# Attention in blocks that may span two units: the value bank and the spare bank change roles from unit to unit

## The chip, the cores and the metric

One Trainium2 chip, one of its cores. The metric is the device time of one execution in microseconds (us); the lower the better. A core has a matrix engine (TensorE, PE in the profile; its weight loads are listed apart as PEld), a vector engine (VectorE, DVE), an activation engine (ScalarE, ACT), GpSimd (POOL) and the engine that issues most transfers (SyncE, SP). Each runs its own instructions in their order; they meet at semaphores. Matmuls write to PSUM, which has 8 banks of 128 partitions x 512 floats.

## The reference

The program normalises 2048 rows of 512 numbers, runs full attention with 32 heads of 16 dimensions over them, runs a SwiGLU feed-forward network over the same normalised rows, and uses the network's output as a gate on the attention's.

```python
xn = layernorm(x)                                   # 2048 x 512
q, k, v = split(xn @ wqkv)                          # 32 heads of 16
p = softmax(q @ k.T * 16 ** -0.5)                   # 2048 x 2048 for each head
s = (p @ v) @ wo
g = silu((silu(xn @ w_gate) * (xn @ w_up)) @ w_down)   # inner width 1792
return x + s * g
```

## The kernel before

All of it is one function, `tile_block`, whose instructions are issued in a hand-written order. A first stage (some 163 us) normalises the rows, makes queries, keys and values and stores them in DRAM, in two parts each, a rounded value and the rest, so that single-pass float32r matmuls keep float32 accuracy. Then come the 32 **units** of attention. A unit is one group of four heads (of 8) and one block of 512 queries (of 4); `u = 4 * group + block`. It runs over 16 key tiles (`kt`) of 128 keys. For each key tile there are two **pairs** of heads. A pair's scores are two matmuls of 50 rows, one on the upper and one on the lower half of the array, which run side by side.

- A **direct** pair writes both halves to one of two score tiles in PSUM (`scored`); ScalarE takes the exponential from there (line 966). Two score tiles mean that the third pair waits until the first's exponential is done.
- A **copied** pair writes one half at a time to a single spare PSUM bank (`spare_bank`, which is `acc[1]`); VectorE copies each half to SBUF (lines 1022 and 1028) and ScalarE takes the exponential there, at the end (line 1036). Its two halves are the events A and B of the block's order.

Between the scores the matrix engine does **fills**: `fill(1)` takes the next step of the feed-forward network (later of the output projection) from a queue, two matmuls of 64 rows side by side into the banks `bankx` and `banky` (line 188, later 381). The exponentials of a pair take longer than its scores, and the fills use that time.

The order is cut in **blocks**. A block has so many key tiles, so many fills and, behind them, one section of `values` (line 410): the products of the block's exponentials with the values, four heads side by side in the array's four column groups, added up over the unit in the PSUM bank `acc[0]`. The blocks' fills (`sizes`) are 24 or 21, as the network's chains of 3 x 8, 3 x 7 come, so that a chain ends with its block; 88 of the entries belong to the network, the last 8 to the output projection. Before the change a block belongs to one unit. There are three blocks for each unit, 96 in all, with 5, 6 and 5 key tiles as a rule (the six where the fills are many). To make it come out even, two of the 24-step chains are parted into two blocks of 12 fills and 4 tiles, one at units 22/23 and one at units 30/31. Their first two pairs are issued ahead (`begin`), inside the previous block's values, so that the values come in two pieces there: 100 sections of values for 96 blocks.

`events(n, f, ...)` writes down a block's order of fills (F), direct pairs (D) and copied halves (A, B), for instance `DDFAFFFFDFFBDFFFDFFAFDFFFDFBFDFFFDFFFD` for 6 tiles and 24 fills: 10 direct and 2 copied pairs. There are four common forms, named here by fills/direct/copied: 24/10/2 (6 tiles), 24/9/1 (5 tiles), 21/8/2 (5 tiles), 21/9/3 (6 tiles). `run` issues the block. Small VectorE work (rounding of weights and the like) waits in the list `chores` and is issued between the copies where there is room.

When a unit's last values are done, `finish` has VectorE transpose `acc[0]` to SBUF (`turn`, line 421), invert the sums (line 426) and scale (line 430). It is queued after the second pair of the next block. Nothing but the next unit's own values, a whole block later, needs the bank that the transpose reads. SP loads the queries of unit u+1 when unit u begins (`load_q`, `load_shift`), and the next group's keys and values in a ring of five buffers as its chunks come free.

After the last block the projection of the last queries ends the kernel.

Of the kernel before, what the change touches and what calls it, by code (L numbers as in the profile page):

```python
# [9 lines left out]
F32 = mybir.dt.float32  # L10
# [36 lines left out]
PARTED = (22, 23)  # L47
# [5 lines left out]
def tile_block(ctx: ExitStack, tc: tile.TileContext, x, wqkv, wo, w_gate, w_up, w_down, out):  # L53
# [301 lines left out]
    def out_splits():  # L355
        for b, c in {early: ((0, 0), (0, 1), (0, 2)), early + 2: ((1, 0), (1, 1)), early + 3: ((1, 2), (2, 0)),
                     early + 4: ((2, 1),), early + 5: ((2, 2),)}.get(now, ()):
# [48 lines left out]
    def values(u, kts, probs):  # L406
        for kt in kts:
            v = vst[(u // NB * NB + kt // CT) % RING]
            for h in range(4):
                mm(acc[0][h * 32:h * 32 + DH + 1], v[:, kt % CT, h * (DH + 1):(h + 1) * (DH + 1)],  # L410
                   probs[kt, h // 2][:, h % 2], start=kt == 0, stop=kt == KT - 1, skip_group_check=True)

    def normalise(u, first, last, between=None):
        g, b = divmod(u, NB)
        n = last - first
        turned = {}
        dst = on[b][:, first:last].rearrange("p (c s d) -> p c s d", s=2, d=DH)[:, :, g % 2]

        def turn():
            turned[0] = late.tile([P, TB], F32, tag="o", name="o")[:, :n]  # L420
            dve.transpose(turned[0], acc[0][:, first:last])
# [74 lines left out]
    blocks, opened = [], []  # L496
    for u in range(units):
        opened.append(len(blocks))
        if u == 0:
            ns = [4, 6, 6]  # L500
        elif u in PARTED or u >= units - 2:
            ns = ([4, 6, 6] if u % 2 else [6, 6, 4])
        else:
            ns = [5] * 3
            far = sizes[len(blocks):len(blocks) + 3]
            ns[far.index(max(far)) if far[1] < max(far) else 1] = 6
        kt = 0
        for n in ns:
            blocks.append((u, kt, n))
            kt += n  # L510

    def events(n, f, ahead):
        length = 2 * n - ahead + f
        need = 2 * n - max(2, (10 * length + 46) // 40)
        fit = (10 * length + 55) // 112
        copied = n - 3 if ahead else max(0, min(need, fit)) if now else 0
# [3 lines left out]
        ds = [] if ahead else [0, 1]  # L520
        ds += [(0.5 if ahead else 7) + gap * i for i in range(direct - 2)]
        cs = [((0.3 if ahead else 2.2) + far * i, "AB"[i % 2]) for i in range(2 * copied)]
# [421 lines left out]
    spare_bank = acc[1]  # L944
# [24 lines left out]
    begun = {}  # L969

    def begin(u, first, n):
        for j in range(2):
            begun[first, j] = scored(u, j, first, j)

    def run(u, first, n):
        nonlocal lower
        f = sizes.pop(0) if sizes else 0
        direct, todo = events(n, f, len(begun))
# [3 lines left out]
        if now >= early and f != pair // 2:  # L982
# [3 lines left out]
        pairs = [(kt, j) for kt in range(first, first + n) for j in range(2)]  # L986
        straight, copies = pairs[:direct], pairs[direct:]
        probs, waiting, turned_in = {}, [], []

# [5 lines left out]
        done = len(begun)  # L995
        if done:
            probs.update(begun)
            begun.clear()
            unit_end()
        copying = [t + 1.5 for t, e in todo if e in "AB"]  # L1000
        final = max(at for at, (_, e) in enumerate(todo) if e == "F")
        free = 0
        for at, (t, e) in enumerate(todo):
# [4 lines left out]
            elif e == "D":  # L1008
                probs[straight[done]] = scored(u, done % 2, *straight[done])
# [3 lines left out]
            elif e == "A":  # L1013
# [3 lines left out]
                kt, j = copies.pop(0)  # L1017
                waiting.append((kt, j))
                scores(u, spare_bank, kt, j, 0)
                lower = True  # L1020
                probs[kt, j] = ppool.tile([P, 2, TB], F32, tag="pr", name="pr")
                dve.tensor_copy(probs[kt, j][:, 0], spare_bank)  # L1022
                free = copying.pop(0) + 3
            else:
                kt, j = waiting[-1]
                scores(u, spare_bank, kt, j, 1)
                lower = False
                dve.tensor_copy(probs[kt, j][:, 1], spare_bank)  # L1028
# [6 lines left out]
        for kt, j in waiting:  # L1035
            act(probs[kt, j], probs[kt, j], AF.Exp, scale=0.25)  # L1036
# [5 lines left out]
        kts = range(first, first + n)  # L1042
        if now + 1 in begins:
            values(u, kts[:-1], probs)
            begin(*blocks[now + 1])
            values(u, kts[-1:], probs)
        else:
            values(u, kts, probs)

    for now, (u, first, n) in enumerate(blocks):  # L1050
        g, b = divmod(u, NB)
        if first == 0 and 0 < u < units - 1:
            load_q(u + 1)
            load_shift(u + 1)
        if now == 3 or first == 0 and 0 < g < NG - 1 and b == 0:
            load_k(g + 1, 0)
            load_v(g + 1, 0)
        run(u, first, n)
# [6 lines left out]
        if b == NB - 1 and g + 1 < NG:  # L1065
            for c in range(NB - 1):
                if first < (c + 1) * CT <= first + n:
                    load_k(g + 1, c + 1)
                    load_v(g + 1, c + 1)
        if first + n == KT and u + 1 < units:  # L1070
            ends.append(partial(finish, u))
# [7 lines left out]
    outs = (score[0][:, 0], score[1][:, 0], spare_bank, bankx)  # L1079
# [73 lines left out]
```

## Time and profile before

| | |
|---|---|
| median of 3 runs | 1393.43 us (1393.23 to 1393.66) |
| the profiled execution's own time | 1393.85 us |
| its span, first to last instruction | 1392.1 us |
| TensorE busy | 1386.0 us (100%) |
| ScalarE busy | 1087.5 us (78%) |
| VectorE busy | 757.7 us (54%) |
| granted TensorE clock | 0.999 |

The profiled execution is 0.42 us above the median of the runs, and its span is 1.75 us shorter than its own time. The page gives busy time for each engine, the chain of work that ended last, and the costliest groups of instructions. Since matmuls are pipelined and two or four of them run side by side, a TensorE that is busy all the time can still lose time between its instructions; what counts is when each section of the order starts. The chain of waits, in order of time, lists each section of values as one piece with its start, so that the distance from one section to the next is the length of a block.

### The profile page before, as it was taken

Reading aid. Unit: us, or ns where it says so; the run is one execution under the profiler, and the core shown is the slowest. Engines: PE = TensorE matmul, PEld = TensorE weight load, DVE = VectorE, ACT = ScalarE, POOL = GpSimd, SP = SyncE. Lnnn points to the kernel's source line nnn. Section 1 sums busy time; section 2 is a strip of 40 time slices with the busy share of each in tenths; the row PEclk is TensorE's granted clock in tenths of the full one; section 3 lists DMA queues with packets and bytes.
Section 4 is the critical chain, followed back from the end, with each engine's and each line's share of the span. In section 5 each row is a group of like instructions: output and inputs, shape, how many; then the busy total and the mean of one; then the engine's idle time right before and its main releaser. Section 6 shows DMA issues by size and latency. Waiting matters only on the chain.

```text
span 1392.1 us, 27644 instructions
## 1 busy us (share of the span) xinstructions
PE 1386.0 (100%) x11193; PEld 850.6 (61%) x11193; DVE 757.7 (54%) x1295; ACT 1087.5 (78%) x1245; POOL 74.4 (5%) x92
## 2 busy tenths in 40 slices
PE   9999999999999999999999999999999999999998
PEld 7777756655655655565556566555655565565665
DVE  6675555355545653555456544564555446556544
ACT  6753678778888877887887787788888887788785
POOL 4200200000000000000000000000000000000222
PEclk9999999999999999999999999999999999999999
DMA  7778641043534511144524402347124212224323
GB/s 228 269 247 267 175 109 43 13 113 88 127 91 115 122 44 36 47 127 98 131 62 108 104 13 63 84 128 163 50 66 116 54 27 70 82 81 151 125 82 138
DMA packets 126954, 148.15 MB, mean 106 GB/s; under 512 B 12524, under 2 KB 79340, under 8 KB 126052
## 3 DMA queue, kind: packets, MB, share of 16 engines
q1 hardware_dynamic: 121620, 125.79, 33.9%
q0 software_dynamic: 4912, 20.12, 3.9%
q8 instruction: 90, 1.47, 0.4%
q14 instruction: 44, 0.36, 0.1%
q10 hardware_dynamic: 288, 0.39, 0.1%
HBM read 106.68 MB, written 39.58 MB: 105 GB/s over the span
## 4 chain that ended last, share of the span: by engine, by line
PE 88%; ACT 0%; DVE 0%; issue 0%; DVEq 0%
PE acc L410 32%; PE bankx L188 23%; PE score L960 17%; PE banky L188 10%; PE acc L960 3%; PE bankx L381 2%; PE banky L381 1%; ACT pr L966 0%; PE acc L1090 0%; PE bankx L1090 0%; PE score L1090 0%; DVE y L1097 0%; DVE y L1103 0%; DVEq L1149 0%
## 5 line engine op out<-in xcount | busy, mean ns | idle before, releaser
L966 ACT ACTIVATE pr<-score 128x1024 f32<-128x1024 f32 x859 | 812.5, 1031 | 222.6 <-PE score L960 221.3
L410 PE MATMUL acc<-pr,vst 128*17 128x512 f32 x4096 | 459.0, 593 | 0.0
L960 PE MATMUL score<-qst,kst 50*128 50x512 f32 x1718 | 394.4, 413 | 0.1
L188 PE MATMUL bankx<-fx,guh 64*128 64x512 f32 x896 | 332.0, 393 | 0.1
L188 PE MATMUL banky<-fx,guh 64*128 64x512 f32 x896 | 323.3, 393 | 0.0
L410 PEld LDWEIGHTS acc<-pr,vst 128*17 128x17 f32 x4096 | 110.1, 97 | 290.8 <-issue 269.2
L960 PEld LDWEIGHTS score<-qst,kst 50*128 50x128 f32 x1718 | 175.1, 184 | 143.8 <-issue 70.6
L1022 DVE COPY pr<-acc 128x512 f32<-128x512 f32 x165 | 114.1, 692 | 186.8 <-PE acc L960 183.8
L188 PE MATMUL bankx<-wd,hh 64*128 64x512 f32 x672 | 199.5, 392 | 0.0
L188 PE MATMUL banky<-wd,hh 64*128 64x512 f32 x672 | 197.0, 391 | 0.0
L188 PEld LDWEIGHTS bankx<-fx,guh 64*128 64x128 f32 x896 | 166.5, 186 | 21.1 <-issue 2.6
L188 PE MATMUL banky<-fx,gul 64*128 64x512 f32 x448 | 175.5, 392 | 0.0
L188 PE MATMUL bankx<-fx,gul 64*128 64x512 f32 x448 | 175.2, 391 | 0.0
L188 PEld LDWEIGHTS banky<-fx,guh 64*128 64x128 f32 x896 | 166.4, 186 | 5.2
L1036 ACT ACTIVATE pr<-pr 128x1024 f32<-128x1024 f32 x165 | 168.8, 1077 | 0.0
L1028 DVE COPY pr<-acc 128x512 f32<-128x512 f32 x165 | 114.0, 691 | 75.1 <-PE acc L960 61.8
L188 PEld LDWEIGHTS bankx<-wd,hh 64*128 64x128 f32 x672 | 125.0, 186 | 12.1
L241 DVE SCALAR_TENSOR_TENSOR ga<-th,bankx 128x512 f32<-128x512 f32 x56 | 38.5, 688 | 171.5 <-ACT th L240 171.4
L960 PE MATMUL acc<-qst,kst 50*128 50x512 f32 x330 | 130.8, 396 | 0.0
L188 PEld LDWEIGHTS banky<-wd,hh 64*128 64x128 f32 x672 | 124.9, 186 | 3.8
L188 PEld LDWEIGHTS bankx<-fx,gul 64*128 64x128 f32 x448 | 83.6, 187 | 10.9
L188 PEld LDWEIGHTS banky<-fx,gul 64*128 64x128 f32 x448 | 83.5, 186 | 2.7
(186 smaller groups left out, 1297.9 us busy)
## 6 DMA issues: line engine op xcount, KB each, us to landing
gur<-in_B_w_gate_dram SPq DMA_DIRECT2D x56, 256.0 KB
gur<-in_B_w_up_dram SPq DMA_DIRECT2D x56, 256.0 KB
wdr<-in_B_w_down_dram SPq DMA_DIRECT2D x56, 256.0 KB
kst<-k_d SPq DMA_DIRECT2D x192, 64.0 KB
qst<-q_d SPq DMA_DIRECT2D x192, 64.0 KB
fx<-xt_d SPq DMA_DIRECT2D x24, 512.0 KB
q_d<-parts SPq DMA_DIRECT2D x16, 512.0 KB
k_d<-parts SPq DMA_DIRECT2D x16, 512.0 KB
```

What stands on the lines that cost most here:

```text
L188: mm(banks[i], lhs[halves[i]], rhs[halves[i]], start=start, stop=stop)
L241: dve.scalar_tensor_tensor(ga, th, 1.0, bankx, op0=ALU.add, op1=ALU.mult)
L381: mm(banks[k], lhs[b, c][a][halves[h], (j + k) * P:(j + k + 1) * P], fx[halves[h], w, c], start=swap == i == 0, stop=i == 3 * n - 1, skip_ ...
L410: mm(acc[0][h * 32:h * 32 + DH + 1], v[:, kt % CT, h * (DH + 1):(h + 1) * (DH + 1)], probs[kt, h // 2][:, h % 2], start=kt == 0, stop=kt = ...
L960: mm(bank, k[r, j, kc * P:(kc + 1) * P], qst[u % 2][r, j], start=True, stop=True)
L966: act(pr, score[slot], AF.Exp, scale=0.25)
L1022: dve.tensor_copy(probs[kt, j][:, 0], spare_bank)
L1028: dve.tensor_copy(probs[kt, j][:, 1], spare_bank)
L1036: act(probs[kt, j], probs[kt, j], AF.Exp, scale=0.25)
```

## The change

- **Blocks** are made from the list of fills alone: 6 tiles where there are 24 fills, otherwise 5, with some of the sixes turned to fives so that the sum is 512 tiles; the first three and the last three have 4, 6 and 6. A block takes its tiles from wherever the previous one stopped, so that it may hold the last tiles of one unit and the first of the next: `blocks` is now a list of lists of parts `(u, first, n)`. Neither chain is parted any more: 94 blocks, 25 of which span two units. `begin` and `PARTED` are gone.
- **Banks**: unit u adds up its values in `acc[u % 2]`, and the spare bank for copied pairs is the other one, chosen by the unit with which the block begins. So the bank that held a finished unit's values is the spare bank of the next blocks.
- **finish** issues the transpose at once instead of putting it in the list of chores, since the first copied half of that block writes over the bank.
- **events**: in the block behind a unit's end (`late`) the first copied half stands 5 steps in instead of 2.2: `DDFFFAFF...` instead of `DDFAFFFF...`. The special case for parted blocks is gone.
- The loads of a unit's successor's queries and of the next group's first keys go out behind the block in which the unit begins, where that block spans two units. The splits of two output operands come in one block instead of two.

```diff
-PARTED = (22, 23)
...
-                mm(acc[0][h * 32:h * 32 + DH + 1], v[:, kt % CT, h * (DH + 1):(h + 1) * (DH + 1)],
-                   probs[kt, h // 2][:, h % 2], start=kt == 0, stop=kt == KT - 1, skip_group_check=True)
+                mm(acc[u % 2][h * 32:h * 32 + DH + 1], v[:, kt % CT, h * (DH + 1):(h + 1) * (DH + 1)],
+                   probs[u, kt, h // 2][:, h % 2], start=kt == 0, stop=kt == KT - 1, skip_group_check=True)
...
-            dve.transpose(turned[0], acc[0][:, first:last])
+            dve.transpose(turned[0], acc[u % 2][:, first:last])
...
-        chores.extend(normalise(u, 0, TB))
+        (_, turn), *rest = normalise(u, 0, TB)
+        turn()
+        chores.extend(rest)
...
-    sizes[3 * PARTED[0] + 2:3 * PARTED[1]] = [3 * DC // 2] * 2
...
-    sizes += [6 * (DT - 1), pair, pair, pair, pair // 2, pair // 2, pair, pair]
-    begins = tuple(3 * u + i for a in (PARTED[0], units - 2) for u, i in ((a, 2), (a + 1, 0)))
...
+    sizes += [6 * (DT - 1)] + [pair] * (2 * (NB - 1))
+
+    ns = [6 if f == max(sizes) else 5 for f in sizes]
+    ns[:3] = ns[-3:] = [4, 6, 6]
+    long = [i for i, n in enumerate(ns) if n == 6 and 3 <= i < early]
+    over = sum(ns) - units * KT
+    for i in range(over):
+        ns[long[(2 * i + 1) * len(long) // (2 * over)]] = 5
+
+    blocks, opened = [], {}
+    u = kt = 0
+    for n in ns:
+        parts = []
+        while n:
+            some = min(n, KT - kt)
+            if not kt:
+                opened[u] = len(blocks)
+            parts.append((u, kt, some))
+            n -= some
+            kt += some
+            if kt == KT:
+                u, kt = u + 1, 0
+        blocks.append(parts)
...
-        cs = [((0.3 if ahead else 2.2) + far * i, "AB"[i % 2]) for i in range(2 * copied)]
+        ds = [0, 1] + [7 + gap * i for i in range(direct - 2)]
+        cs = [((5 if late else 2.2) + far * i, "AB"[i % 2]) for i in range(2 * copied)]
...
-        direct, todo = events(n, f, len(begun))
+        n = sum(some for _, _, some in parts)
+        direct, todo = events(n, f, bool(ends))
...
+        spare_bank = acc[(parts[0][0] + 1) % 2]
...
-        if now + 1 in begins:
-            values(u, kts[:-1], probs)
-            begin(*blocks[now + 1])
-            values(u, kts[-1:], probs)
-        else:
-            values(u, kts, probs)
...
+        for u, first, some in parts:
+            values(u, range(first, first + some), probs)
...
+        if len(parts) > 1:
+            queries_ahead(parts[1][0])
```

How the instructions move is seen at three places. The first is TensorE's order at unit 22's parted block; `score` are the two score tiles, `acc_80` and `acc_81` the banks `acc[0]` and `acc[1]`, `pr` the exponentials, `vst` the values, `kst` and `qst` keys and queries. Before:

```order
L960 MATMUL score_8971<-qst_557,kst_8975 128x512 x2
L410 MATMUL acc_80<-pr,vst_554 17x512 x8
L410 MATMUL acc_80<-pr,vst_8976 17x512 x12
L960 MATMUL score_8970<-qst_557,kst_8979 128x512 x2
L960 MATMUL score_8971<-qst_557,kst_8979 128x512 x2
L410 MATMUL acc_80<-pr,vst_8976 17x512 x4
L188 MATMUL bankx<-fx,guh 128x512
```

Two pairs of the next block stand between the values of the fifth tile and those of the sixth. With the change, at the end of unit 22 (block 67):

```order
L963 MATMUL score_8971<-qst_8987,kst_549 128x512 x2
L409 MATMUL acc_80<-pr,vst_8980 17x512 x16
L409 MATMUL acc_81<-pr,vst_550 17x512 x8
L963 MATMUL score_8970<-qst_8987,kst_549 128x512 x2
L963 MATMUL score_8971<-qst_8987,kst_549 128x512 x2
L187 MATMUL bankx<-fx,guh 128x512
```

The section of values is in one piece again, and in that one piece unit 22's last four tiles go to `acc_80` and unit 23's first two to `acc_81`.

The second place is TensorE's order behind the end of unit 1, from the end of the values on. Before, with the values in `acc_80` and the spare bank `acc_81`:

```order
L410 MATMUL acc_80<-pr,vst_554 17x512 x4
L960 MATMUL score_8970<-qst_557,kst_553 128x512 x2
L960 MATMUL score_8971<-qst_557,kst_553 128x512 x2
L188 MATMUL bankx<-wd,hh 128x512
L188 MATMUL banky<-wd,hh 128x512
L960 MATMUL acc_81<-qst_557,kst_8975 128x512
```

That is a block inside a unit; before the change the block behind a unit's end has the same order. With the change, behind unit 1's end (unit 1 in `acc_81`, the first tile of unit 2 in `acc_80`):

```order
L409 MATMUL acc_80<-pr,vst_550 17x512 x4
L963 MATMUL score_8970<-qst_557,kst_549 128x512 x2
L963 MATMUL score_8971<-qst_557,kst_549 128x512 x2
L187 MATMUL bankx<-wd,hh 128x512
L187 MATMUL banky<-wd,hh 128x512
L187 MATMUL bankx<-wd,hh 128x512
L187 MATMUL banky<-wd,hh 128x512
L187 MATMUL bankx<-wd,hh 128x512
L187 MATMUL banky<-wd,hh 128x512
L963 MATMUL acc_81<-qst_557,kst_553 128x512
```

The first copied half has moved behind three fills, and it writes the bank that VectorE has to read first.

The third place is VectorE's order at the same sort of block, behind unit 2's end. Before:

```order
L421 STREAM_TRANSPOSE o<-acc_80 128x512
L426 RECIPROCAL rl<-o 128x16
L1022 COPY pr<-acc_81 128x512
L430 TENSOR_TENSOR on_8997<-o,rl 128x16x16
```

With the change:

```order
L420 STREAM_TRANSPOSE o<-acc_80 128x512
L425 RECIPROCAL rl<-o 128x16
L1018 COPY pr<-acc_80 128x512
L429 TENSOR_TENSOR on_8997<-o,rl 128x16x16
```

VectorE's own order is the same; only the bank of the copy is now the one that the transpose has read.

More of the change, by code (lines that the diff above doesn't have):

```diff
@@ L489, in tile_block, with events @@
     sizes = sizes[1:]
-    sizes[3 * PARTED[0] + 2:3 * PARTED[1]] = [3 * DC // 2] * 2
     early = len(sizes)
     pair = 6 * DT
-    sizes += [6 * (DT - 1), pair, pair, pair, pair // 2, pair // 2, pair, pair]
-    begins = tuple(3 * u + i for a in (PARTED[0], units - 2) for u, i in ((a, 2), (a + 1, 0)))
[L496 to L502, printed above, removed]
-        else:
[L504 to L513, printed above, removed]
+    sizes += [6 * (DT - 1)] + [pair] * (2 * (NB - 1))
[19 more added lines that the diff above has]
+        blocks.append(parts)
+    def events(n, f, late):
+        length = 2 * n + f
         need = 2 * n - max(2, (10 * length + 46) // 40)
         fit = (10 * length + 55) // 112
-        copied = n - 3 if ahead else max(0, min(need, fit)) if now else 0
+        copied = max(0, min(need, fit)) if now else 0
         direct = 2 * n - copied
@@ L967, in scored, with run @@
         return pr
[L969 to L975, printed above, removed]
+    def run(parts):
         nonlocal lower
-        f = sizes.pop(0) if sizes else 0
-        direct, todo = events(n, f, len(begun))
+        f = sizes.pop(0)
+        n = sum(some for _, _, some in parts)
+        direct, todo = events(n, f, bool(ends))
         if now == 0:
@@ L981, in run @@
                 todo.insert(0, todo.pop(max(i for i, (_, e) in enumerate(todo) if e == "F")))
-        if now >= early and f != pair // 2:
+        if now >= early:
             behind = [i for i, (_, e) in enumerate(todo) if e == "F"][f // 2]
@@ L1064, in tile_block @@
             load_shift(1)
[L1065 to L1071, printed above, removed]
+        for u, first, some in parts:
+            g, b = divmod(u, NB)
+            if b == NB - 1 and g + 1 < NG:
+                for c in range(NB - 1):
+                    if first < (c + 1) * CT <= first + some:
+                        load_k(g + 1, c + 1)
+                        load_v(g + 1, c + 1)
+            if first + some == KT and u + 1 < units:
+                ends.append(partial(finish, u))
+        if len(parts) > 1:
+            queries_ahead(parts[1][0])
     fill(total)
@@ L1078, in tile_block @@
     lo = one.tile([P, D], F32R, tag="th", name="rl")
-    outs = (score[0][:, 0], score[1][:, 0], spare_bank, bankx)
+    outs = (score[0][:, 0], score[1][:, 0], acc[units % 2], bankx)
     half = TB // 2
```

52 lines of the change are left out of this document (25 added, 27 removed).

## The prediction

> **What bounds the kernel now.** I read the page first, for the engine that is never idle and for the chain, then the chain of waits in order of time, for the length of each block.
>
> ```profile
> span 1392.1 us, 27644 instructions
> ...
> PE 1386.0 (100%) x11193; PEld 850.6 (61%) x11193; DVE 757.7 (54%) x1295; ACT 1087.5 (78%) x1245; POOL 74.4 (5%) x92
> ...
> PEclk9999999999999999999999999999999999999999
> ...
> PE 88%; ACT 0%; DVE 0%; issue 0%; DVEq 0%
> ...
> L966 ACT ACTIVATE pr<-score 128x1024 f32<-128x1024 f32 x859 | 812.5, 1031 | 222.6 <-PE score L960 221.3
> ```
>
> TensorE is busy throughout, at the full clock, and nearly the whole chain is its own. ScalarE waits 221 us for scores, VectorE is idle for 46%. Since matmuls overlap, "busy" hides lost time; I look for it in when things start. First the pace of the order inside a block, from TensorE's timeline:
>
> ```profile
> 353.49 0.39 PE L960 MATMUL score<-qst,kst 50*128 50x512 f32 x2
> ...
> 356.28 0.40 PE L960 MATMUL score<-qst,kst 50*128 50x512 f32 x2
> ```
>
> Between these two pairs lie three rounds of three fills and a pair, 12 steps in 2.79 us: **0.2325 us for a step** (a fill or a pair; a copied half counts a half). Then the values and the blocks, from the chain of waits (start, length, what; x8 is one key tile, x40 five, x48 six):
>
> ```profile
> 241.35 4.42 PE acc L410 x40
> 254.00 5.27 PE acc L410 x48
> ...
> 536.58 4.42 PE acc L410 x40
> 548.54 4.42 PE acc L410 x40
> ...
> 665.03 4.42 PE acc L410 x40
> 677.60 5.27 PE acc L410 x48
> ...
> 729.14 4.42 PE acc L410 x40
> 741.80 4.42 PE acc L410 x40
> ...
> 997.42 5.27 PE acc L410 x48
> 1011.39 5.27 PE acc L410 x48
> 1057.19 5.27 PE acc L410 x48
> 1071.15 5.27 PE acc L410 x48
> ...
> 1300.02 5.27 PE acc L410 x48
> 1314.25 5.28 PE acc L410 x48
> ...
> 1360.50 5.28 PE acc L410 x48
> ```
>
> and, for the parted chain, the same view from 1025 us on:
>
> ```profile
> 1025.36 4.42 PE acc L410 x40
> 1029.78 0.66 PE score L960 x3
> 1030.44 0.98 PE acc L410 x8
> 1031.42 0.43 PE bankx L188
> ...
> 1035.95 2.70 PE acc L410 x24
> ```
>
> One tile of values takes 0.98, six take 5.27: 0.86 each and 0.12 for the section. From the start of one section to the next runs a section of values and the steps of the next block; what is left when 0.86 a tile and 0.2325 a step are taken off is the block's **fixed part**:
>
> - 24/10/2: 1011.39 - 997.42 = 13.97, less 5.16 and 36 steps (8.37): 0.44. With a six before and behind it (1057.19 to 1071.15) it is 13.96, so sixes in a row cost nothing more.
> - 24/9/1: 12.66 - 4.30 - 34 steps (7.91) = 0.45. 21/8/2: 11.96 - 4.30 - 31 steps (7.21) = 0.45.
> - 21/9/3: 12.65 and 12.57, less 4.30 and 33 steps (7.67): 0.68 and 0.60, mean 0.64.
> - 24/10/2 in the output projection: 14.23 - 5.16 - 8.37 = 0.70.
> - The parted chain at units 22/23: 1025.36 to 1057.19 is 31.83 us and holds 14 tiles (12.04) and 20 + 20 + 36 steps (17.67). That leaves 2.12, of which one whole block has 0.44: 1.68 for the two small ones.
> - The parted one at units 30/31: 1314.25 to 1360.50 is 46.25, with 20 tiles (17.20) and 36 + 20 + 20 + 36 steps (26.04): 3.01, less two whole blocks at 0.70: 1.61.
>
> So the kernel is TensorE's work plus some 0.45 us a block.
>
> **The change, part by part.** The work itself stays: 512 tiles, 1024 pairs, the same fills; only their order changes. By the planner's own lists there are now 94 blocks with 94 sections of values, none parted, none 21/9/3; behind block 2 the network's part has 39 of 24/10/2, 32 of 21/8/2 and 15 of 24/9/1.
>
> - Two parted chains become whole blocks: 1.68 - 0.44 = 1.24 and 1.61 - 0.70 = 0.91, saved. One of the last stage's blocks now has no copied pair, which the trace shows only ahead of the first values; its fixed part lies between 0.31 (two bare pairs, 0.66 less two steps, and a section's 0.12) and 0.70. I take 0.70, that of its neighbours, whose banks turn over in the same way.
> - Five blocks of 21/9/3 become 21/8/2: 5 x (0.64 - 0.45) = 0.95, saved.
> - The rest of the blocks swap forms with the same 0.44 to 0.45: nothing.
> - 859 direct pairs become 855 and 165 copied ones 169. TensorE's steps are the same. VectorE gets 8 copies of 0.69 more, 5.5 us over the span in 46% idle time; without that cover they would cost those 5.5.
> - Transpose and spare bank: the first copied half behind a unit's end now waits for the transpose. What stands there before:
>
> ```profile
> 348.32 0.61 PE L410 MATMUL acc<-pr,vst 128*17 128x512 f32 x4
> 348.87 0.73 PE L960 MATMUL score<-qst,kst 50*128 50x512 f32 x4
> 349.43 0.40 PE L188 MATMUL bankx<-fx,guh 64*128 64x512 f32 x1
> ...
> 349.67 0.39 PE L960 MATMUL acc<-qst,kst 50*128 50x512 f32 x1
> ...
> 347.75 0.69 DVE L144 TENSOR_TENSOR hh<-ga,hh 128x512 fp32r<-128x512 f32 x1
> 349.06 0.72 DVE L421 STREAM_TRANSPOSE o<-acc 128x512 f32<-128x512 f32 x1 [0.61 <-PE acc L410]
> ```
>
> The values end at 348.93, the transpose starts 0.13 later and ends at 349.78. Left at 349.67 the copied half would be late; behind three fills it is due at 349.43 + 3 x 0.2325 = 350.13, its weights a step earlier, at 349.90. With the same 0.13 from VectorE back to TensorE the release comes at 349.91. So it is on time to within 0.01 us. It is also the worst case: where the block spans two units, the next unit's tiles (0.86 each) stand between the last values and this block, and the transpose runs that much earlier, for VectorE is idle for 0.61 ahead of it. With the sharing as planned, 25 of the 31 ends are of that kind, one has no copies behind it, and 5 are bare. What queues behind a late half is everything: the fills, then the next pair, then ScalarE. For the five I bound the cost by 0 and 0.2 each (0 to 1.0) and take 0.15 in all, near the lower end, to which the rows point.
> - The first copied half 2.8 steps later, in 30 blocks:
>
> ```profile
> 349.50 8.36 ACT L966 ACTIVATE pr<-score 128x1024 f32<-128x1024 f32 x9 [2.82 <-PE score L960]
> ```
>
> ScalarE takes 0.93 an exponential, four steps, and starts each block from idle. The new orders keep the direct pairs 3.5 to 4.5 steps apart, as those of 21/8/2 do, and their last pair stands where it stood. Bounds: 0, and the excess of the crowded 21/9/3, 0.19 each, 5.7 in all; I take 0, since the spacing is 21/8/2's.
> - The loads behind the block instead of ahead of it:
>
> ```profile
> 498.32 2.66 SPq L100 DMA_DIRECT2D qst<-q_d  x6
> 501.02 0.86 SPq L113 DMA_DIRECT2D qst<-sh_d  x2
> ```
>
> SP spends 3.5 us on issuing a unit's queries. They are needed after at least 11 more tiles, two blocks or some 24 us. Nothing; if they were late, the first pair of a unit would wait.
>
> Sum: 1.24 + 0.91 + 0.95 - 0.15 = 2.95, say **3.0 us less**. The profiled execution's 1393.85 would be 1390.9; its median lies 0.42 lower, so 1393.43 - 3.0 = **1390.4 us**.
>
> **Rivals.** *Only the section's switch is saved.* The remaining 0.32 of a block's fixed part could belong to its pairs, as ScalarE's pace, and travel with them to other blocks. Then six sections fewer give 6 x 0.12 = 0.7: 1392.7 us. Against it: the small block's 18 steps from 1031.42 to 1035.95 take 4.53, 0.34 over 18 x 0.2325, the same as in a block with twice the steps. The Trainium skill ("TensorEngine Tiling (Array Packing)", Key Properties) says that a change of the tiling mode drains the array, and "TensorE: Matmul & The Clock Gate" (Step-by-step: what each phase is for) puts a drain at some 128 cycles; as an estimate from these pages, at 2.4 GHz, that is 0.05 us, two a block, and 0.64 us for six blocks, so this rival's result. The trace's 0.12 a section agrees in size, but the 0.45 a block goes beyond it.
>
> *The copied half waits at every unit's end* (slower). If VectorE gets to the transpose late, because the previous block's rounding work still stands ahead of it, TensorE stops at 30 places. A block in which TensorE had to wait for ScalarE shows a price:
>
> ```profile
> 560.75 1.39 PE acc L410 x9
> ```
>
> From 548.54 it is 12.21 to here, where the same form took 11.96: 0.25. Thirty times that is 7.5, and the time 1393.43 - 3.0 + 7.5 = 1397.9 us. From 0.10 an end it eats the gain, from 0.19 it is slower by over 0.2%. For it: the margin above, which is nothing. Against it: VectorE's last instruction ahead of the transpose ends at 348.44, half a microsecond early. The Trainium skill ("TensorE: Matmul & The Clock Gate", The mechanism) has matmuls strictly in program order, which is why one late half would hold up all of them; in these rows nothing passes a waiting matmul either.
>
> *The later copies crowd the block's end* like 21/9/3: 5.7 - 3.0 = 2.7 more, 1396.1 us. Against it stands the spacing.
>
> *The change does nothing*: excluded, as the order of instructions shows whole sections across units and no parted block.
>
> **How the numbers follow.** The forecast 0.68, with a range of its own from 1389.4 (no wait at the ends, 0.15; the block without copies at its lower bound, 0.39; and two disturbed blocks like the one at 548.54 gone, 0.5) to 1391.3 (the five ends at 0.2); only the switch 0.20; the wait at every end 0.08; the crowding 0.04. About 0.2% (2.8 us) is what a measurement of this kernel can tell from no change, so "faster" needs less than 1390.6, hardly above the forecast; with a sum of bounds that lean both ways I give 0.56 of its 0.68 to faster and 0.12 to within. Together: faster 0.56, within 0.2% 0.32, slower 0.12. The range from 1389.2 to 1393.4 takes in the forecast and the first rival and leaves the other two out.
>
> **What would show it.** Right: 94 sections of values, 0.44 to 0.45 over work in whole blocks, the stretch of units 22 and 23 shorter by 1.2 us, and in the blocks behind a unit's end the same fixed part as elsewhere, with a transpose that ends 0.3 us or more ahead of the first copied half. Wrong: a fixed part of 0.55 or more in those blocks, weight loads of `acc` that wait for VectorE's transpose, ScalarE idle inside a block, or first pairs that wait for a queries' load.

## The result and the profile after

The changed kernel takes **1391.37 us** (median of 22 runs, 1391.05 to 1392.85); the kernel before, run beside it, 1393.62 (22 runs, 1393.19 to 1395.51). The ratio is 0.9984, with a 95% interval from 0.9977 to 0.9991: 2.2 us less (0.16%), where 3.0 were forecast. The profiled execution took 1391.23 us, and that of before 1393.85, so the two traces lie 2.6 us apart, 0.4 more than the medians.

First the page of the changed kernel, the lines that were shown of before (busy us, share of the span, instructions; the granted clock; the chain's shares by engine; the exponentials of the direct pairs):

```profile
span 1389.4 us, 27646 instructions
PE 1381.9 (99%) x11193; PEld 850.6 (61%) x11193; DVE 763.1 (55%) x1303; ACT 1087.8 (78%) x1245; POOL 73.1 (5%) x92
PEclk9999999999999999999999999999999999999999
PE 88%; DVE 0%; DVEq 0%; issue 0%
L969 ACT ACTIVATE pr<-score 128x1024 f32<-128x1024 f32 x855 | 810.5, 1029 | 219.7 <-PE score L963 218.8
```

The span is 2.6 us shorter, as many matmuls as before, at the same clock. VectorE is 5.4 us busier, the eight copies more; ScalarE's 0.3 us is all that else grew. As before, the page cannot say where time went; the lengths of the blocks can. The chain of waits of the changed kernel in order of time (start, length, what), from five places:

```profile
266.25 4.42 PE acc L409 x40
278.19 4.42 PE acc L409 x40
...
1018.92 4.42 PE acc L409 x40
1032.01 5.28 PE acc L409 x48
1045.98 5.27 PE acc L409 x48
...
1302.53 5.27 PE acc L409 x48
1317.52 5.28 PE acc L409 x48
...
1331.78 5.27 PE acc L409 x48
```

With 0.86 us a tile and 0.2325 a step taken off, as in the prediction, the fixed parts are these. Around units 22 and 23, where the parted chain stood: 13.09 - 4.30 - 8.37 = 0.42, and 13.97 - 5.16 - 8.37 = 0.44. Behind a bare unit's end, one with which the block before ended as well (266.25 to 278.19): 11.94 - 4.30 - 7.21 = 0.43. These are as forecast (0.44 to 0.45). In the output projection, 1302.53 to 1317.52 gives 14.99 - 5.16 - 8.37 = **1.46**, and the next block 0.73. The 1.46 is the one block that went wrong: the third of the projection (the second with 24 fills), behind unit 29's end. Before, it had 0.70.

Doing this for every section of both traces and adding up gives the balance (us; the work itself taken off):

| part | before | after | difference | forecast |
|---|---|---|---|---|
| up to the first values | 163.08 | 162.80 | -0.28 | 0 |
| fixed parts in the network's blocks | 39.11 | 36.62 | -2.49 | -2.04 |
| fixed parts in the projection's blocks | 5.62 | 5.47 | -0.15 | -0.91 |
| behind the last values | 12.18 | 12.48 | +0.30 | 0 |
| sum (span) | | | -2.62 | -2.95 |

What stopped that block is seen on VectorE. Its rows in the changed kernel (start, length, engine, line, operation), and TensorE's weight load that waited:

```profile
1310.55 0.71 DVE L447 STREAM_TRANSPOSE o<-on 128x512 f32<-128x512 f32 x1
1311.33 0.69 DVE L1024 COPY pr<-acc 128x512 f32<-128x512 f32 x1
1311.94 0.42 DVE L461 CAST wd<-o 128x512 fp32r<-128x512 f32 x1
1312.39 0.69 DVE L458 TENSOR_TENSOR wd<-o,wd 128x512 fp32r<-128x512 f32 x1
1313.00 0.14 DVE L384 COPY turned_over<-bankx 1x1 f32<-1x1 f32 x1
```

```profile
1313.26 0.18 PEld L380 LDWEIGHTS banky<-fx,part 64*128 64x128 f32 x1 [0.88 <-DVE turned_over L384]
```

In the projection, the fills of one output block end in the middle of a block; two one-element VectorE copies (`turned_over`, line 384) hand the banks over, and the next fill may only start behind them. With the first copied half 2.8 steps later, the second one is later as well, and the last two chores of the unit's end (the cast and the subtraction, 1.1 us) stand behind it and ahead of the hand-over. TensorE waits 0.88. Before, the same two chores ended in time:

```profile
1308.79 0.41 DVE L460 CAST wd<-o 128x512 fp32r<-128x512 f32 x1
1309.23 0.69 DVE L457 TENSOR_TENSOR wd<-o,wd 128x512 fp32r<-128x512 f32 x1
1309.84 0.14 DVE L385 COPY turned_over<-bankx 1x1 f32<-1x1 f32 x1
```

From the block's first pair to the hand-over it was 4.61 us (from 1305.23) and is now 5.27 (from 1307.73).

### The profile page after: what moved, and what is told of

It reads as the page before. It is cut to its first block, busy times and chain, and to the rows that moved or that the text cites. A ratio compares the mean times of both kernels' runs of the same rounds, so it can differ in the third digit from the quotient of the medians.

```text
span 1389.4 us, 27646 instructions
## 1 busy us (share of the span) xinstructions
PE 1381.9 (99%) x11193; PEld 850.6 (61%) x11193; DVE 763.1 (55%) x1303; ACT 1087.8 (78%) x1245; POOL 73.1 (5%) x92
## 3 DMA queue, kind: packets, MB, share of 16 engines
q8 instruction: 89, 1.46, 0.4%
## 4 chain that ended last, share of the span: by engine, by line
PE 88%; DVE 0%; DVEq 0%; issue 0%
PE acc L409 32%; PE bankx L187 25%; PE score L963 17%; PE banky L187 8%; PE acc L963 3%; PE bankx L380 2%; PE banky L380 1%; PE acc L1092 0%; PE bankx L1092 0%; PE score L1092 0%; DVE y L1099 0%; DVE wd L458 0%; DVE pr L1024 0%; DVE y L1105 0%; DVE wd L461 0%; DVE turned_over L384 0%
## 5 line engine op out<-in xcount | busy, mean ns | idle before, releaser
L963 PE MATMUL score<-qst,kst 50*128 50x512 f32 x1710 | 399.7, 412 | 0.0
L187 PE MATMUL bankx<-fx,guh 64*128 64x512 f32 x896 | 325.1, 393 | 0.1
L187 PE MATMUL banky<-fx,guh 64*128 64x512 f32 x896 | 319.2, 393 | 0.0
L963 PEld LDWEIGHTS score<-qst,kst 50*128 50x128 f32 x1710 | 178.4, 184 | 141.8 <-issue 78.2
L1018 DVE COPY pr<-acc 128x512 f32<-128x512 f32 x169 | 116.9, 691 | 236.5 <-PE acc L963 235.7
L1032 ACT ACTIVATE pr<-pr 128x1024 f32<-128x1024 f32 x169 | 172.3, 1078 | 0.0
L1024 DVE COPY pr<-acc 128x512 f32<-128x512 f32 x169 | 116.8, 691 | 78.8 <-PE acc L963 67.6
```

Of the source, the lines that this page charges most:

```text
L187: mm(banks[i], lhs[halves[i]], rhs[halves[i]], start=start, stop=stop)
L963: mm(bank, k[r, j, kc * P:(kc + 1) * P], qst[u % 2][r, j], start=True, stop=True)
L1018: dve.tensor_copy(probs[u, kt, j][:, 0], spare_bank)
L1024: dve.tensor_copy(probs[u, kt, j][:, 1], spare_bank)
L1032: act(probs[u, kt, j], probs[u, kt, j], AF.Exp, scale=0.25)
```

## The experiments

Below, "over its steps" is a block's time from its first pair to its values, less 0.2325 us a step; the section of values adds 0.12 to make the fixed part.

**The changed kernel again**, on the same chip as the next three. The later ones ran on two other chips, each beside the kernel before, which took 1393.75 us here and 1393.90 and 1393.85 there. So where a time is set against the 1391.59 of this run, 0.1 to 0.2 us of the difference may be the chip's.

> The changed kernel again, beside the next three on the same chip. Both theories: 2.0 to 2.8 us below the kernel before, and 1.2 to 1.4 us of fixed part in the one projection block behind the end of unit 29 (block 89, the second half of the first output block), where its neighbours have 0.5 to 0.6.

1391.59 us (1391.31 to 1391.90; ratio to before 0.9981, interval 0.9972 to 0.9990). The block behind unit 29's end is at 1.38 over its steps again (1.35 in the first trace): it belongs to the program, not to one execution.

**The two chores held back behind the hand-over**, in that block alone.

```diff
+        fills = 0
...
                 fill(1)
+                fills += 1
...
-            while chores and at < final and (not copying or
+            while chores and at < final and not (now == early + 2 and 8 <= fills < 12) and (not copying or
```

> Theory: block 89 loses 0.8 us because VectorE hands the banks over in the middle of the projection only after a cast and a subtraction that the unit's end put ahead of it. Held back until the twelfth fill is issued, they leave the hand-over free: block 89's fixed part falls from 1.35 to 0.5 to 0.65 us, every other block stays, and the time is 0.7 to 0.9 us below the changed kernel. Rival: the later copied half and the exponentials behind it are what TensorE waits for there; then block 89 keeps at least 1.2 us and the time stays within 0.2 us.

1390.95 us (ratio 0.9979, 0.9970 to 0.9988), 0.64 less than the changed kernel beside it, a little under the 0.7 to 0.9 that I expected (the spans of the traces: 1389.1 and 1389.8). The runs of this kernel spread widely, from 1390.67 to 1392.42 us, so the block in the trace is better evidence than the time: it falls to 0.65. VectorE's rows in this kernel:

```profile
1311.73 0.69 DVE L1026 COPY pr<-acc 128x512 f32<-128x512 f32 x1
1312.65 0.14 DVE L384 COPY turned_over<-bankx 1x1 f32<-1x1 f32 x1 [0.23 <-PE bankx L380]
...
1312.79 0.41 DVE L461 CAST wd<-o 128x512 fp32r<-128x512 f32 x1
1313.23 0.69 DVE L458 TENSOR_TENSOR wd<-o,wd 128x512 fp32r<-128x512 f32 x1
```

Now VectorE waits for TensorE's last fill ahead of the hand-over (0.23), not the other way round. The order of two chores, on an engine that is 55% busy, was worth 0.7 us of the block.

**More room for chores ahead of the first copied half**: behind a unit's end that lies inside the block before, they may start after one step instead of 4.5.

```diff
-        free = 4.5 if ends else 0
+        free = 0 if not ends else 4.5 if parts[0][1] == 0 else 1
```

> Behind an end that lies inside a block the transpose is over before the next block begins, so the scaling and the second transpose may go ahead of the first copied half, where VectorE is idle. Theory: block 89 falls to 0.5 to 0.65 us as in the experiment before, by filling idle time instead of holding work back, and the other blocks behind such ends stay at 0.30 us of scoring overhead: 0.7 to 0.9 us below the changed kernel. Rival: work ahead of the copied half holds it up at these 25 places by 0.05 to 0.2 us each: 1 to 5 us above the changed kernel.

1391.78 us (ratio 0.9983, 0.9974 to 0.9992): no gain. The cast and the subtraction did move ahead, but two chores of the next operand filled their place:

```profile
1312.19 0.42 DVE L1030 CAST wd<-wd 128x512 fp32r<-128x512 f32 x1
1312.65 0.69 DVE L329 TENSOR_TENSOR wd<-wd 128x512 fp32r<-128x512 f32 x1
1313.26 0.14 DVE L384 COPY turned_over<-bankx 1x1 f32<-1x1 f32 x1
```

The hand-over came 5.30 us after the block's first pair, no earlier than 5.27. So it is not these two chores that matter but that any 1.1 us of VectorE work stands there. My expectation was wrong, and so was the rival: the blocks behind the other ends did not get longer.

**The first copied half early again, everywhere** (2.2 steps), with the new banks.

```diff
-        cs = [((5 if late else 2.2) + far * i, "AB"[i % 2]) for i in range(2 * copied)]
+        cs = [(2.2 + far * i, "AB"[i % 2]) for i in range(2 * copied)]
```

> The first copied half behind a unit's end goes back to 2.2 steps, so that it has to wait for the transpose where that ends 0.9 us into the block. Theory: only the five ends that fall on a block's end are bare, and cost 0.25 to 0.35 us each (1.3 to 1.7 us); behind the 25 others the transpose is over before the block begins and they cost nothing; block 89 is back at 0.55 to 0.65 us (0.8 us less). Net 0.4 to 1.0 us above the changed kernel. Rival, the wait at every end: 30 times 0.3 us, 9 us above.

1391.50 us (ratio 0.9980, 0.9971 to 0.9989), the same as the changed kernel, where I had expected 0.4 to 1.0 more. The five blocks behind a bare unit's end each take 0.25 to 0.28 us more (0.55 to 0.60 over their steps where their like have 0.30 to 0.32), 1.3 in all, and the block behind unit 29's end is back at 0.57, 0.8 less. That leaves 0.5, which smaller differences from the changed kernel's trace beside it cancel. The block behind unit 5's end falls from 0.52 to 0.35 (the last experiment tells why), and behind the other ends that lie inside a block the times agree to within 0.05. The first block of the projection, with 18 fills, takes 0.65 instead of 0.51. Up to the first values it is 0.2 more, behind the last ones 0.3 less, and over the network's other blocks some 0.4 less in bits of 0.05 or under. These were not looked into. At a bare end, VectorE's and TensorE's rows of this kernel are

```profile
271.42 0.72 DVE L420 STREAM_TRANSPOSE o<-acc 128x512 f32<-128x512 f32 x1 [3.02 <-PE acc L409]
```

```profile
272.19 0.18 PEld L963 LDWEIGHTS acc<-qst,kst 50*128 50x128 f32 x1 [0.43 <-DVE o L420]
```

and in the changed kernel

```profile
270.79 0.72 DVE L420 STREAM_TRANSPOSE o<-acc 128x512 f32<-128x512 f32 x1 [3.01 <-PE acc L409]
```

```profile
271.41 0.19 PEld L187 LDWEIGHTS bankx<-wd,hh 64*128 64x128 f32 x1
...
271.65 0.18 PEld L963 LDWEIGHTS acc<-qst,kst 50*128 50x128 f32 x1
```

With the early half, the weights wait 0.43 for the transpose and load 0.05 behind its end (271.42 + 0.72 = 272.14). With the late one, they load 0.14 behind its end (271.51) and wait for nothing: 0.09 in hand.

**One more section of values in each of 86 blocks**: the first tile ahead of the block's last fill, the rest behind.

```diff
+                if at < final or now == 0 or now >= early:
+                    fill(1)
-                fill(1)
...
+            if i == 1 and 0 < now < early:
+                fill(1)
...
+            values(u, (kt,), probs)
```

> In the blocks 1 to 86 the last fill stands behind the first tile of the block's values instead of ahead of them, so that each of the 86 has one more section of values and one more of scoring. Theory, the fixed part belongs to the sections: 0.12 us for the values and 0.15 to 0.2 us for the return, 23 to 28 us above the changed kernel. Rival, only a drain at each change of shape: two times 0.05 us, 9 us above. Rival, the fixed part belongs to the pairs: nothing but the section's 0.12 us, 10 us above.

1428.77 us (two runs; ratio 1.0249, 1.0230 to 1.0267), 37.2 more than the changed kernel and more than the theory's 28. The chain of waits of this kernel shows one such place, a tile alone, a fill alone, five tiles:

```profile
309.57 0.98 PE acc L409 x8
310.55 0.42 PE bankx L187
310.98 4.42 PE acc L409 x40
```

The extra section costs 0.98 - 0.86 = 0.12, and the single fill takes 0.42 instead of 0.23, 0.20 more: 0.32 together, 27.6 us for 86. That part is in the theory's range; 9 to 10 us, the rivals, are rejected. The rest lies in the 39 blocks of 24/10/2, which are 0.2 longer each (0.52 over their steps, not 0.32), some 8 us. There the last direct pair now stands right ahead of the values without a fill between them; that this is the reason was not tried. The Trainium skill ("TensorEngine Tiling (Array Packing)", Key Properties) says that a change of the tiling mode drains the array; these rows agree so far as each change costs time, without showing that it is a drain. They put two changes at 0.32 us, three times the 0.11 that the prediction's estimate from the Trainium skill's pages gives for two.

**The late order alone, in the kernel before.**

```diff
-        cs = [((0.3 if ahead else 2.2) + far * i, "AB"[i % 2]) for i in range(2 * copied)]
+        cs = [((0.3 if ahead else 5 if late else 2.2) + far * i, "AB"[i % 2]) for i in range(2 * copied)]
...
-        free = 0
+        free = 4.5 if ends else 0
...
-        chores.extend(normalise(u, 0, TB))
+        (_, turn), *rest = normalise(u, 0, TB)
+        turn()
+        chores.extend(rest)
```

> The kernel before, with one thing of the change: behind a unit's end the first copied half stands 5 steps in, the transpose goes out at once, and the work behind it is counted from there. Banks and blocks are as before. Theory: the later order costs nothing in the network's blocks and 0.7 to 0.8 us in the one projection block behind unit 29's end, 0.7 us above the kernel before in all. Rival, the later copies crowd the end of 30 blocks by 0.19 us each: 5.7 us above.

1395.55 us against 1393.9 (ratio 1.0012, 1.0002 to 1.0021): 1.65 slower. The network's whole blocks keep their medians (0.32 for 24/10/2, 0.30 for 24/9/1, 0.31 for 21/8/2). The block behind unit 29's end goes from 0.58 to 1.41, with the same wait on TensorE:

```profile
1311.17 0.18 PEld L381 LDWEIGHTS banky<-fx,part 64*128 64x128 f32 x1 [0.91 <-DVE turned_over L385]
```

So the order alone does this, without the new banks and blocks. The rest I had not foreseen: the two small blocks behind a unit's end, with only 12 fills, go from 0.40 and 0.39 to 0.89 and 0.90, 0.5 more each.

**Twenty blocks of 21 fills with six tiles** (21/9/3), twenty of 24 with five in exchange.

```diff
+    for i in [i for i, f in enumerate(sizes) if f == 21][:20]:
+        ns[i] = 6
-    long = [i for i, n in enumerate(ns) if n == 6 and 3 <= i < early]
+    long = [i for i, n in enumerate(ns) if n == 6 and 3 <= i < early and sizes[i] == 24]
```

> The changed kernel with twenty of the 21-fill blocks at 6 tiles (21/9/3) and as many of the 24-fill blocks at 5. Theory: 0.19 us for each crowded block, 3.8 us above the changed kernel. Rival, the excess belonged to the places where the five stood: within 0.5 us.

1399.74 us (ratio 1.0040, 1.0026 to 1.0053), 8.15 more than the changed kernel, twice what I expected. Fourteen of the twenty are near 0.53 (0.47 to 0.59), 0.22 more than 21/8/2, where the prediction's term has 0.19. The other six, at 1.10 to 1.22, are those behind a unit's end. With three copied pairs in 21 fills and the first half late, the halves follow each other as fast as the spare bank is read out, and TensorE waits for VectorE's copy:

```profile
241.70 0.18 PEld L965 LDWEIGHTS acc<-qst,kst 50*128 50x128 f32 x1 [0.53 <-DVE pr L1020]
```

So the third rival's mechanism exists; in the changed kernel no block has the form that it needs.

**Four of the network's chains parted** into 12 fills and 4 tiles twice, without pairs issued ahead.

```diff
+    for i in (66, 46, 24, 12):
+        sizes[i:i + 1] = [12, 12]
...
-    ns = [6 if f == max(sizes) else 5 for f in sizes]
+    ns = [6 if f == max(sizes) else 4 if f == 12 else 5 for f in sizes]
```

> The changed kernel with four of the network's 24-fill chains parted into two blocks of 12 fills and 4 tiles, without pairs ahead: 98 blocks. Theory: each costs one more block's fixed part (0.44 us) and, since six exponentials of 0.93 us do not fit into 20 steps of 0.2325 us, up to 0.9 us for each small block: 2 to 9 us above the changed kernel, near 5 if it is as much for each chain as the parted chain cost before (1.24 us over a whole one). Rival, only the section's switch: 4 times 0.12 us, 0.5 us above.

1402.11 us (ratio 1.0057, 1.0044 to 1.0071), 10.5 more than the changed kernel, 2.6 a chain and above the 9 that I had as the upper end. Of the eight small blocks, six stand near 0.70 over their steps and the two behind a unit's end at 1.99; the sections of values take 4.4 us more than in the changed kernel, as they wait for exponentials that are not done. The parted chain of before at units 22/23 had cost 1.2; there two pairs of each small block were issued ahead and one was copied instead of two. Which of the two makes the difference was not tried.

**The late order only at the five bare ends**, the version that the runs so far pointed to.

```diff
-        direct, todo = events(n, f, bool(ends))
+        direct, todo = events(n, f, bool(ends) and parts[0][1] == 0)
```

> The whole computation; the first copied half stays five steps into the block only where the block before ended exactly with a unit (five blocks); where the unit's end lies inside the block before, it goes back to 2.2 steps. Theory (the late order is needed only at the five bare ends; behind the other 25 it gains nothing and in the output projection it pushes the mid-block hand-over back): the block behind unit 29's end falls from 1.35 over its steps to about 0.56 (-0.8), the five bare ends stay at 0.29 to 0.32, all else unchanged: 0.8 us below the changed kernel, some 1390.7 to 1390.9. Rival (the later copies pay somewhere else, for instance by room for VectorE's other work behind spanning ends, as the near-equal times of the changed kernel and of the one with early halves everywhere could suggest): no difference from the changed kernel, 1391.5.

**1390.61 us** (1390.17 to 1391.13; ratio to before 0.9977, 0.9967 to 0.9986), the fastest kernel of the study: 1.0 below the changed kernel's 1391.59 and 3.2 below before's 1393.85 beside it. The two kernels' intervals against before overlap, so it is the blocks that tell: the one behind unit 29's end is at 0.56, the five bare ends stay at 0.29 to 0.35, the one behind unit 5's end falls to 0.36, and the first block of the projection rises to 0.65, which I had not foreseen. VectorE and TensorE behind unit 29's end:

```profile
1312.14 0.43 DVE L461 CAST wd<-o 128x512 fp32r<-128x512 f32 x1
1312.48 0.14 DVE L384 COPY turned_over<-bankx 1x1 f32<-1x1 f32 x1
...
1313.33 0.68 DVE L458 TENSOR_TENSOR wd<-o,wd 128x512 fp32r<-128x512 f32 x1
```

```profile
1312.68 0.18 PEld L380 LDWEIGHTS bankx<-fx,part 64*128 64x128 f32 x1 [0.16 <-DVE turned_over L384]
```

The wait of 0.88 is one of 0.16.

**One ScalarE instruction more**, of one column, 2 us into the program, on the changed kernel. This concerns a smaller riddle: two blocks of the changed kernel and two of before, not the same ones, are 0.2 to 0.3 us longer than their like, because an exponential starts late with its scores done. Rows of ScalarE, of the changed kernel and of before:

```profile
466.65 5.64 ACT L969 ACTIVATE pr<-score 128x1024 f32<-128x1024 f32 x6 [2.82 <-PE score L963]
472.57 2.85 ACT L969 ACTIVATE pr<-score 128x1024 f32<-128x1024 f32 x3 [0.28 <-ACT pr L969]
```

```profile
712.25 3.77 ACT L966 ACTIVATE pr<-score 128x1024 f32<-128x1024 f32 x4 [0.27 <-ACT pr L966]
```

```diff
         act(root, root, AF.Sqrt)
+        act(root, root, AF.Sqrt)
```

> The changed kernel with a single 128x1 ScalarE instruction more, at 2 us, where ScalarE is idle. In every trace so far the exponentials of the network's blocks that started late with their scores done stood at ScalarE instruction 574 and 702 (changed) or 446, 830 and 1086 (before), all 62 over a multiple of 128. Theory (every 128th ScalarE instruction starts up to 0.28 us late, and this costs where it is an exponential in the middle of a block): the late exponentials move by one instruction: those at 393 and 472 us go, and since by the changed kernel's list some nine of the places now fall on an exponential in the fourth to ninth place of a block, those blocks gain 0.2 to 0.28 each: 1.0 to 2.0 us slower than the changed kernel. Rival (the late exponentials belong to these blocks' data or their order of work): the same blocks late, no other, and no difference in time.

1391.91 us (ratio 0.9986, 0.9977 to 0.9995), 0.3 above the changed kernel's 1391.59, within what the two runs' intervals leave open. The two late exponentials are gone, and two others have come, at 550 and 941 us, again at ScalarE instructions (830 and 1470, counted from 0 with the waits for semaphores among them) that are 62 over a multiple of 128:

```profile
466.72 8.50 ACT L970 ACTIVATE pr<-score 128x1024 f32<-128x1024 f32 x9 [2.78 <-PE score L964]
...
545.07 4.73 ACT L970 ACTIVATE pr<-score 128x1024 f32<-128x1024 f32 x5 [2.48 <-PE score L964]
550.05 2.86 ACT L970 ACTIVATE pr<-score 128x1024 f32<-128x1024 f32 x3 [0.26 <-ACT pr L970]
```

So the place in ScalarE's stream decides, not the block alone. That nine blocks would suffer was wrong: of the nine exponentials that now stand at such a place, two start more than 0.06 us late.

The traces also show why so few do. Right ahead of most exponentials ScalarE has a record of its own, the wait for the scores. In the twelve traces such a wait stands at 61 over a multiple of 128 at 59 places, and at each of them the instruction behind it starts 0.34 us or more after the wait; elsewhere in the attention, when ScalarE was free, that takes 0.06 to 0.07. So the pause is there each time, and shows only where ScalarE would have been free within it. In the changed kernel's block behind unit 5's end the wait stands at 392.78 and the exponential before it ends at 392.94: the next starts at 393.12. In the best version the scores come earlier in the block, the wait stands at 392.88 and the exponential before it ends at 393.21: the next starts at 393.23, and the block is 0.18 shorter.

## Why the prediction came out as it did

The forecast of 1390.4 us was 1.0 too low; the measured 1391.37 lies just above the 1391.3 to which the forecast's own range reached. A gain of more than 0.2%, to which I gave 0.56, did not come; 0.16% did ("within 0.2%" had 0.32). Luck helped: between the traces the miss is 0.3, although one block lost 0.77, because the network gained 0.45 more than forecast, and for 0.30 of that I have no cause. Step by step:

- **The parted chain at units 22/23, 1.24 forecast: right.** Before, its two small blocks and the pairs issued ahead have 1.14 over their steps, and four sections of values 0.47; a whole block has 0.43 in all. That is 1.18 saved.
- **The parted chain in the projection, 0.91: right in size, hidden by a loss.** Leaving out the block behind unit 29's end, which went from 0.58 to 1.35 over its steps and so lost 0.77, the projection gained 0.15 + 0.77 = 0.92. The block without copied pairs has 0.73 (0.62 over its steps), where I took 0.70.
- **21/9/3 to 21/8/2, 0.95: right.** Over their steps the five have 0.51 on average before, 21/8/2 now has 0.31: five times 0.20 is 1.0. The crowded kernel confirms the price (0.22 each away from a unit's end).
- **The five bare ends, 0.15: they cost nothing.** I had the transpose's end (0.91 after the block's first pair) and the copied half's place (1.26) right to 0.01, but took the 0.13 that it takes from TensorE to VectorE for the way back as well. The early halves show 0.05 for that, at all five ends. This accounts for 0.15 of the network's 0.45 over the forecast; the rest is shared out over the blocks at 0.01 or less each, and I have no cause for it. (The prediction counts its forms "behind block 2"; they are those of the blocks 1 to 86, which changes no sum. And the two disturbed blocks whose end would have made its range lower did not go: two others are as long now.)
- **"The first copied half 2.8 steps later, in 30 blocks: I take 0": the step that failed.** It holds for 28 of the 30. In the one behind unit 29's end it costs 0.77, since the chores behind the later second half run into the hand-over of the banks. I had asked what the later half does to ScalarE and the pairs' spacing. I did not ask which VectorE work is pushed back, nor who waits for that, although the hand-over was in the code and its rows in the trace of before. The kernel with the chores held back, the one with early halves, the late order in the kernel before and the best version all show it. The other exception, behind unit 5's end, loses 0.2: the later half pushes a pair's scores back, and there ScalarE's pause is no longer hidden. With either alone the block has 0.29 (late order, the pause moved by one instruction) or 0.35 to 0.36 (early order, the pause in place), with both 0.52 to 0.54.
- **Loads and copies at nothing: right.** VectorE's 5.4 us more, as forecast (5.5), and the blocks in which a unit begins keep the length of their like, so no first pair waited for its queries.
- **0.28 less up to the first values and 0.30 more behind the last** cancel; neither was in the sum, and their causes were not looked into. The changed kernel's second trace has 162.94 up to the first values instead of 162.80, so about half of the 0.28 is one execution's chance.

Of the rivals, **"only the section's switch"** would have left 0.7 of gain; the blocks' other fixed part does go with the block (0.32 for one more section with a fill behind it, 1.2 for the parted chain at units 22/23). **The wait at every unit's end** did not happen: no weight load of a copied half waits for the transpose in the changed kernel. The 0.25 that the prediction read off the block at 548.54 and took as its price is ScalarE's pause (instruction 830), not a wait of that kind; a copied half that is too early costs 0.25 to 0.28, as the early halves show. **The crowding** did not happen in the changed kernel's forms, but starts as soon as three copied pairs stand in 21 fills.

## What to carry to other kernels

When an order is shifted to make room for one dependence, list everything that is queued behind the shifted instructions on each engine, and look for the one consumer that is on the critical path: here 28 places had slack, one lost a little, and one was a hand-over that TensorE waits for. A margin that is computed as zero deserves a measured latency in each direction, not the same one twice. And a special order should stand only where its reason holds: confined to the five bare ends, it kept their gain without the loss behind unit 29's end.

## What the hardware showed that I had not expected

- **ScalarE pauses at fixed places of its stream.** In the traces of before and of the changed kernel, every exponential of the network's blocks that starts more than 0.1 us late with its scores done (up to 0.28) is the instruction numbered 62 over a multiple of 128 among ScalarE's records (446, 830, 1086 before; 574 and 702 in the changed kernel), and one instruction more at the start moved it to other blocks. The pause is there at every such place where it can be seen (0.34 us from the wait to the instruction behind it, at 59 places in twelve traces, instead of 0.06), and most places show no delay because ScalarE is still busy with the exponential before. What ScalarE does in the pause was not shown.
- **A single fill between two sections of values costs 0.42 us instead of 0.23**, and the section itself 0.12: 0.32 for going in and out, three times the prediction's estimate from the Trainium skill's pages.
- **The way from VectorE to TensorE is short**: 0.05 us from the end of the transpose to the weight load that waited for it, against 0.13 from the last matmul's end, which the profile models, to the transpose's start.
